# Scores of two heads as float32 products in halves of TensorE's rows, without split keys and queries

## The chip, the cores and the metric

The kernel runs on one core of a Trainium2 chip. A core has TensorE (PE: an array of 128 rows and 128 columns, fed with weights by PEld), VectorE (DVE), ScalarE (ACT), GpSimd (POOL), and DMA queues, which here are all issued by SyncE (SP). The metric is the time on the device in microseconds, and fewer is better. A difference is told in percent of the kernel before.

## The reference

Attention over 2 batches, 8 heads, 576 positions and 64 channels, in which each query keeps only its 32 largest scores, then two feed-forward layers on the 1152 x 512 result, all in float32:

```python
scores = scale * np.matmul(q, k.transpose(0, 1, 3, 2))
kth = np.partition(scores, -top_k, axis=-1)[..., -top_k:-top_k + 1]
scores = np.where(scores >= kth, scores, -1000000000.0)
attn = np.exp(scores - np.max(scores, axis=-1, keepdims=True))
attn = attn / (np.sum(attn, axis=-1, keepdims=True) + 1e-09)
x = np.matmul(attn, v)                 # then (batch x position) x (head x channel)
h = x @ w_in;  x = (h * np.tanh(softplus(h))) @ w_out        # 512 -> 2048 -> 512
h = x @ w2_in; x = (h * sigmoid(h)) @ w2_out                 # 512 -> 2048 -> 512
```

The feed-forward weights come as float64, so they have to be turned into float32 on the chip.

## The kernel before

**Tiles.** The 1152 rows are 9 tiles of 128. Attention goes by tile and by pair of heads, so there are 36 pairs. Tile 4 holds the end of batch 0 and the start of batch 1, so its scores have two parts.

**One pair.** Scores (L391) go to PSUM in four pieces, one for each head and each half of the 576 keys (288 columns), each piece in one of two banks (`ps_att`, `att=2`). ScalarE or VectorE copies a piece into `sc` (L295, L297). VectorE finds the 32 largest of a row by four MAX8 (L407) and three MATCH_REPLACE8 (L410) a head. ScalarE takes the exponential (L423, or L433 and L440 in the last tiles), L427 masks it. TensorE transposes the result (L452, also in `ps_att`), ScalarE copies it to `pt`, and the value products follow (L468 and L471, `ps_misc`): each head writes 64 of the 128 PSUM partitions, that is, it uses 64 columns of the array. L485 turns the reciprocal denominators and L494 multiplies by them into `xt`.

**How scores are made.** A float32 product is two records on TensorE, a product of the shorter type `float32r` one. To keep float32's precision with the shorter type, keys and queries are split in two parts, a rounded one and the remainder. Keys are loaded twice, one copy above the other (`kraw`, both halves of the 128 partitions), copied as `float32r` by ScalarE or VectorE into `kk`, and in the lower 64 partitions the remainder replaces the copy (GpSimd or VectorE, `kraw` minus `kk`). Queries are loaded the same way (`qraw`) and become two tiles in `qs`, rounded and remainder. A product over 128 rows then sums the query part times both key parts, and two products, one for each query part, give one piece of scores:

```python
ops = [(T[K("qs", i)][:, x, h], T["kk", b, p][:, h]) for i, (b, _, _) in enumerate(pp) for x in range(2)]
for i, (l, r) in enumerate(ops):
    nc.tensor.matmul(o, lhsT=l, rhs=r[:, f * SH:(f + 1) * SH], start=(i == 0), stop=(i == len(ops) - 1))
```

In tile 4 each part has its own `qs`, cleared by GpSimd outside its rows (L373), so a piece takes four products. Keys are prepared once for a batch and a pair (8 times), queries 36 times.

**Feed-forward.** Weights arrive as float64 in `wide`, and ScalarE (L519, L531) and GpSimd (L523, L533) make float32 of them in `wraw`. Tiles 0, 1 and 2 go through layer 1 in float32 (`BLOCK1`, mode 'n'), the others in pairs of tiles with split operands (mode 'r'); layer 2 is the same but for tiles 0 and 1 taken together. L735 and L644 are the first products of a layer (`ps_h`), L714 and L821 the second (`ps_y`). Weights are split into `ws` by copy and subtraction (L295, L297, L303, L305).

**The order.** Every step is given to `Plan.add` with the engines that may do it, a cost, and a rank. Ranks come from tables: `TILES` (start and step of a tile's four pairs), `DUE1` and `DUE2` (of the groups of the layers), `OFF` and `FLEX` (offsets for each kind of step and for taking an alternative engine). `Plan.emit` goes through them with its own costs, keeps count of the buffers (`SBUF_BUFS`, `PSUM_BUFS`), and writes each engine's instructions in the order found. On the chip every engine then runs its own list in that order, and waits where what it needs is not there.

## Time and profile before

| | |
|---|---|
| Time, median of 3 runs | 646.25 us (643.49 to 648.09) |
| The profiled execution | 642.01 us, its span 640.2 us |
| TensorE clock granted, mean | 0.989 |
| Busy share: TensorE / its weight loads | 93% / 82% |
| Busy share: VectorE / ScalarE / GpSimd | 82% / 74% / 53% |
| DMA | 178.34 MB, mean 279 GB/s |

The profile shows one execution. "Busy" is the time in which an engine had an instruction running; on TensorE, products are pipelined, so the price of one in a stream is the distance from its start to the next one's, and its own duration is longer. Idle time is given with its releaser: the instruction whose end the waiting one had needed. A float32 product stands as two records (in the order of the program below it is one MATMUL). L numbers are lines of the kernel that ran.

### The profile page before, as it was taken

How to read it: one execution, taken by the hardware profiler on the slowest of the kernel's cores; microseconds unless marked ns; L12 is line 12 of the kernel's file. 1: busy time of each engine (PE TensorE's matmuls, PEld its weight loads, DVE VectorE, ACT ScalarE, POOL GpSimd, SP SyncE). 2: the span in 40 equal slices, each digit the busy share in tenths (PEclk: the TensorE clock that was granted, in tenths of full speed). 3: DMA queues.
4: the chain of work that ended last, by engine and by line, in shares of the span. 5: the costliest groups of instructions: out<-in, count | busy, mean ns of one | idle time of the engine just before them, and what ended most of it. 6: DMA issues, size and time to landing. Idle time of an engine off the chain costs nothing.

```text
span 640.2 us, 13237 instructions
## 1 busy us (share of the span) xinstructions
PE 592.8 (93%) x4616; PEld 527.9 (82%) x4616; DVE 528.0 (82%) x1121; ACT 476.9 (74%) x991; POOL 338.0 (53%) x319
## 2 busy tenths in 40 slices
PE   1587739999999999999999999999999999999997
PEld 1476629999998966788999778999998999989986
DVE  4999999997999999789999989999996244755541
ACT  6899999897699999988997767996895344333321
POOL 6788886671367877877877426448782000000000
PEclk9998988999999999999999999999999999999999
DMA  9978886997798978999799697959669888887661
GB/s 307 298 226 275 278 251 208 341 335 233 237 326 267 309 247 264 302 370 357 266 383 369 219 341 275 317 164 343 223 221 346 329 306 307 284 253 266 238 193 70
DMA packets 85650, 178.34 MB, mean 279 GB/s; under 512 B 8144, under 2 KB 29136, under 8 KB 85584
## 3 DMA queue, kind: packets, MB, share of 16 engines
q1 hardware_dynamic: 85584, 177.50, 81.7%
q8 instruction: 36, 0.59, 0.4%
q14 instruction: 30, 0.25, 0.1%
HBM read 138.94 MB, written 38.54 MB: 277 GB/s over the span
## 4 chain that ended last, share of the span: by engine, by line
PE 73%; ACT 13%; DMA 7%; DVE 4%; POOL 1%; issue 1%; SPq 0%; POOLq 0%; ACTq 0%; DVEq 0%
PE ps_h L644 26%; PE ps_y L714 16%; PE ps_y L821 15%; PE ps_att L391 5%; PE ps_misc L468 5%; ACT ws L519 4%; PE ps_att L452 4%; DMA w2i<-wraw 2%; ACT wraw L531 2%; DVE m L407 2%; DMA wide<-in_w1o_dram 2%; DVE rest L410 2%; DMA qraw<-in_qh_dram 1%; ACT sc L295 1%; ACT pt L295 1%
## 5 line engine op out<-in xcount | busy, mean ns | idle before, releaser
L407 DVE MAX8 m<-rest 128x8 f32<-128x576 f32 x216 | 154.2, 745 | 0.1
L410 DVE MATCH_REPLACE8 rest<-m,rest 128x576 f32<-128x576 f32 x144 | 106.1, 741 | 0.0
L295 ACT CAST ws<-wraw 128x512 fp32r<-128x512 f32 x98 | 60.1, 622 | 55.8 <-PE ps_h L644 25.9
L519 ACT ACTIVATE ws<-wide,zone 128x512 int32<-128x512 int16 x128 | 95.2, 783 | 2.0 <-POOL wraw L533 1.3
L533 POOL TENSOR_TENSOR wraw<-wraw,ws 128x512 int32<-128x512 int32 x64 | 81.6, 1283 | 15.0 <-ACT wraw L531 3.1
L391 PE MATMUL ps_att<-kk,qs 128*128 128x288 f32 x320 | 67.7, 334 | 22.9 <-POOL kk L303 18.5
L523 POOL TENSOR_TENSOR ws<-ws 128x512 int32<-128x512 int32 x64 | 81.8, 1289 | 9.5 <-ACT ws L519 6.3
L303 POOL TENSOR_TENSOR ws<-wraw,ws 128x512 fp32r<-128x512 f32 x52 | 66.6, 1296 | 26.2 <-DVE ws L297 7.4
L391 PEld LDWEIGHTS ps_att<-kk,qs 128*128 128x128 f32 x320 | 49.1, 198 | 32.0 <-POOL kk L303 20.1
L644 PEld LDWEIGHTS ps_h<-y,ws 128*128 128x128 f32 x576 | 72.8, 188 | 3.0 <-issue 0.2
L644 PE MATMUL ps_h<-y,ws 128*128 128x256 f32 x576 | 75.0, 279 | 0.0
L644 PE MATMUL ps_h<-xt,ws 128*128 128x256 f32 x576 | 70.8, 279 | 0.0
L714 PE MATMUL ps_y<-g,ws 128*128 128x256 f32 x540 | 70.1, 280 | 0.0
L644 PEld LDWEIGHTS ps_h<-xt,ws 128*128 128x128 f32 x576 | 68.1, 188 | 0.8 <-issue 0.6
L305 DVE TENSOR_TENSOR ws<-wraw,ws 128x512 fp32r<-128x512 f32 x57 | 41.5, 734 | 30.2 <-ACT ws L295 29.8
L714 PEld LDWEIGHTS ps_y<-g,ws 128*128 128x128 f32 x540 | 65.3, 188 | 0.7 <-issue 0.7
L821 PE MATMUL ps_y<-ws,g 128*128 128x512 f32 x252 | 65.4, 398 | 0.0
L714 PE MATMUL ps_y<-hs,wraw 128*128 128x128 f32 x384 | 51.6, 282 | 7.6 <-ACT bias L419 7.6
L407 DVE MAX8 m<-sc 128x8 f32<-128x576 f32 x72 | 53.0, 746 | 4.2 <-ACT sc L295 4.1
L452 PE MATMUL ps_att<-ident,e 128*128 128x128 f32 x324 | 51.7, 286 | 3.9 <-DVE e L427 2.8
L714 PEld LDWEIGHTS ps_y<-hs,wraw 128*128 128x128 f32 x384 | 48.2, 198 | 8.3 <-POOL wraw L533 7.7
L410 DVE MATCH_REPLACE8 rest<-m,sc 128x576 f32<-128x576 f32 x72 | 53.1, 740 | 0.0
(90 smaller groups left out, 1147.7 us busy)
## 6 DMA issues: line engine op xcount, KB each, us to landing
wraw<-w1i SPq DMA_DIRECT2D x64, 256.0 KB, 4.5
wraw<-w2i SPq DMA_DIRECT2D x64, 256.0 KB, 3.9
ws<-w1o_split SPq DMA_DIRECT2D x30, 512.0 KB, 5.6
ws<-w2o_split SPq DMA_DIRECT2D x28, 512.0 KB, 4.6
wraw<-w1o SPq DMA_DIRECT2D x48, 256.0 KB, 4.9
wide<-in_w1i_dram SPq DMA_DIRECT2D x16, 512.0 KB, 5.6
wide<-in_w1o_dram SPq DMA_DIRECT2D x16, 512.0 KB, 5.0
wide<-in_w2i_dram SPq DMA_DIRECT2D x16, 512.0 KB, 4.8
```

Of the source, the lines that this page charges most:

```text
L295: ways.append(("act", act_us(n, psum), act, lambda: nc.scalar.copy(get_out(), get_in())))
L303: ways.append(("pool", pool_us(n), pool, lambda: nc.gpsimd.tensor_tensor(out=get_out(), in0=get_a(), in1=get_b(), op=op)))
L391: nc.tensor.matmul(o, lhsT=l, rhs=r[:, f * SH:(f + 1) * SH], start=(i == 0), stop=(i == len(ops) - 1))
L407: add([("dve", 0.67, 0, lambda i=i, h=h, src=src: nc.vector.max(out=m8()[:, h, 8 * i:8 * i + 8], in_=src()[:, h]))], reads=srck, writes=[K ...
L410: add([("dve", 0.73, 0, lambda i=i, h=h, src=src: nc.vector.match_replace(out=rest()[:, h], in_to_replace=m8()[:, h, 8 * i:8 * i + 8], in_ ...
L452: nc.tensor.transpose(o[:, i, :], ef[:, (c + i) * P:(c + i + 1) * P], ident)
L519: add([("act", act_us(UNIT) + 0.14, 0, lambda i=i: nc.scalar.activation(pn()[:, i], top(), AF.Relu, scale=ONE16 - 2 * ONE16 * i, bias=zone))],
L523: ways = [("pool", pool_us(UNIT), 0, lambda: nc.gpsimd.tensor_tensor(out=se(), in0=pn()[:, 0], in1=pn()[:, 1], op=ALU.subtract))]
L533: add([("pool", pool_us(UNIT), 0, lambda: nc.gpsimd.tensor_tensor(out=w().bitcast(I32), in0=w().bitcast(I32), in1=se(), op=ALU.add))], rea ...
L644: nc.tensor.matmul(hp[:, c, :], lhsT=l, rhs=rr, start=(i == 0), stop=(i == len(ops) - 1))
L714: nc.tensor.matmul(yp[:, o, :], lhsT=l[:, d * P:(d + 1) * P], rhs=rr[:, c, :], start=(fc == 0 and k == 0 and o == 0), stop=last, skip_grou ...
L821: nc.tensor.matmul(op, lhsT=gg[:, c, i * P:(i + 1) * P], rhs=wt, start=(fc == 0 and k == 0), stop=(fc == NFC - 1 and k == len(ops) - 1))
```

## The change

Keys and queries are no longer split. Queries are loaded once as `q`, 128 partitions: the 64 channels of one head above those of the other. Keys likewise (`kk`, 128 x 576). The tiles `kraw`, `qraw` and `qs` and all steps that filled them are gone: the key and query casts, subtractions, and the clearing for tile 4. The scores of half a row of keys are now one step for both heads: head 0 as a float32 product of the upper 64 rows of the array, head 1 of the lower 64, each into a bank of its own, so one step takes both `ps_att` banks. In tile 4 each part is a product that writes only its own rows of the bank. `sc` has six buffers instead of four, `ws` nine instead of eight. All numbers that set the order are new, and so are the charges of a score step and of a feed-forward product.

```diff
-TILES = [(-38.49, 10.5), (10.1, 9.21), (77.14, -12.91), (164.62, 9.79), (162.43, 9.24), (220.65, 45.49), (300.21,
...
+TILES = [(2.7, 15.05), (53.05, -1.62), (84.54, -8.19), (202.03, -14.5), (188.75, 19.51), (283.83, -8.15), (312.51,
...
-SBUF_BUFS = dict(kraw=1, kk=5, v=5, qraw=2, qs=2, sc=4, rest=1, e=1, pt=2, m8=10, bias=10, den=8, x=3, dt=2, xt=1,
-    wraw=9, ws=8, hs=2, th=1, wide=3, g=3, y=2, o=2)
+SBUF_BUFS = dict(kk=5, v=5, q=3, sc=6, rest=1, e=1, pt=2, m8=10, bias=10, den=8, x=3, dt=2, xt=1, wraw=9, ws=9, hs=2,
+    th=1, wide=3, g=3, y=2, o=2)
...
-            add(copy_ways(S, hi, src, dve="khi", twice=True), reads=[raw + (h,)], writes=[kk + (h, 0)], uses=U,
-                rank=rank - 6, boost="k")
-            add(tt_ways(S, lo, lambda h=h: T[raw][D:, h], lo, ALU.subtract, dve="klo"), reads=[raw + (h,), kk + (h, 0)], writes=[kk + (h, 1)],
-                uses=U, rank=rank - 6, boost="k")
+        for f in ([0], [1]) if b == 0 and p == 0 else ([0, 1],):
+            cs = slice(f[0] * SH, (f[-1] + 1) * SH)
+            add([("sp", 0.06, 0, lambda cs=cs: nc.sync.dma_start(
+                out=get(kk, lambda: sbuf("kk", [P, S]))[:, cs], in_=kh[b, p][:, cs]))],
+                writes=[kk + (i,) for i in f], uses=[(kk, "kk")], rank=rank - 8, boost="kload", load=len(f) * P * SH * 4)
...
-            add(copy_ways(2 * (r1 - r0), hi, raw, dve="qhi", twice=True), reads=[K("qraw")], writes=[q], uses=U,
-                rank=rank - 6, boost="q")
-            add(tt_ways(2 * (r1 - r0), lo, raw, hi, ALU.subtract, dve="qlo"), reads=[K("qraw"), q], writes=[q], uses=U,
-                rank=rank - 6, boost="q")
+        add([("sp", 0.06, 0, lambda: nc.sync.dma_start(out=get(K("q"), lambda: sbuf("q", [P, P])), in_=qh[t, p]))],
+            writes=[K("q")], uses=[(K("q"), "q")], rank=rank - 8, boost="qload", load=P * P * 4)
...
+        for f in range(2):
+            sp = [K("sp", f, h) for h in range(2)]
+
+            def scores(f=f, sp=sp):
+                for b, r0, r1 in pp:
+                    for h in range(2):
+                        rows = slice(h * D, h * D + D)
+                        nc.tensor.matmul(get(sp[h], lambda: psum("att", [P, SH]))[r0:r1], lhsT=T[K("q")][rows, r0:r1],
+                                         rhs=T["kk", b, p][rows, f * SH:(f + 1) * SH], start=True, stop=True, skip_group_check=True)
+            add([("pe", 0.515, 0, scores)], reads=[K("q")] + [("kk", b, p, f) for b, _, _ in pp], writes=sp, rank=rank - 10,
+                boost="sp", uses=[(k, "ps_att") for k in sp] + [(K("q"), "q")] + [(("kk", b, p), "kk") for b, _, _ in pp])
...
-        native, parts = 0.221 * N / P, 0.354 * N / 256
+        native, parts = (0.2225 if N == P else 0.216 * N / P), 0.3475 * N / 256
```

In the changed kernel the lines have moved up: scores stand at L364, transposes at L424, values at L440 and L443, denominators at L457, and the products of the layers at L707 and L616 (`ps_h`), L686 and L793 (`ps_y`).

The first place is the start of TensorE's list, where the first pairs are made. Before, its first rows are:

```order
L391 MATMUL ps_att<-kk,qs 128x288 x16
L452 MATMUL ps_att<-ident,e 128x128 x9
L485 MATMUL ps_att<-ident,x 128x128
L468 MATMUL ps_misc<-pt,v 64x128 x8
L471 MATMUL ps_misc<-pt,v 64x128 x2
L735 MATMUL ps_h<-xt,wraw 128x128 x4
L391 MATMUL ps_att<-kk,qs 128x288 x4
L735 MATMUL ps_h<-xt,wraw 128x128 x4
L391 MATMUL ps_att<-kk,qs 128x288 x4
```

and now:

```order
L364 MATMUL ps_att<-kk,q 128x288 x8
L424 MATMUL ps_att<-ident,e 128x128 x9
L457 MATMUL ps_att<-ident,x 128x128
L440 MATMUL ps_misc<-pt,v 64x128 x8
L443 MATMUL ps_misc<-pt,v 64x128 x2
L364 MATMUL ps_att<-kk,q 128x288 x2
L707 MATMUL ps_h<-xt,wraw 128x128 x8
L364 MATMUL ps_att<-kk,q 128x288 x2
L707 MATMUL ps_y<-xt,wraw 128x128 x8
```

Both begin with the scores of two pairs; a pair was 8 products and is now 4, two for each half row. Later scores come as bursts of two between the first feed-forward products, where four stood together.

The second place is on TensorE too, where the first layer's first products of tile 1 (L644 before, L616 now, `ps_h`) stand with the second ones of tile 0 (L714, now L686) and the scores of a later pair. Before:

```order
L485 MATMUL ps_att<-ident,x 128x128
L714 MATMUL ps_y<-hs,wraw 128x128 x4
L391 MATMUL ps_att<-kk,qs 128x288 x4
L644 MATMUL ps_h<-xt,wraw 128x128 x4
L391 MATMUL ps_att<-kk,qs 128x288 x4
L714 MATMUL ps_y<-hs,wraw 128x128 x4
L644 MATMUL ps_h<-xt,wraw 128x128 x12
L468 MATMUL ps_misc<-pt,v 64x128 x8
L471 MATMUL ps_misc<-pt,v 64x128 x2
```

and now:

```order
L457 MATMUL ps_att<-ident,x 128x128
L686 MATMUL ps_y<-hs,wraw 128x128 x4
L616 MATMUL ps_h<-xt,wraw 128x128 x4
L364 MATMUL ps_att<-kk,q 128x288 x2
L686 MATMUL ps_y<-hs,wraw 128x128 x4
L616 MATMUL ps_h<-xt,wraw 128x128 x4
L364 MATMUL ps_att<-kk,q 128x288 x2
L616 MATMUL ps_h<-xt,wraw 128x128 x4
L686 MATMUL ps_y<-hs,wraw 128x128 x4
```

The scores were two groups of four, each two pieces of a row of one head; now they are two bursts of two, each half a row of both heads, with full-array products ahead of and behind each. The changed list has 188 borders between products of the whole array, of 64 of its columns (values) and of 64 of its rows (scores), where the one before has 72, all at the value products.

## Rows read from the trace of the kernel before

**Rows 1.** The page's part 1: busy us (share of the span) and instructions of each engine.

```profile
PE 592.8 (93%) x4616; PEld 527.9 (82%) x4616; DVE 528.0 (82%) x1121; ACT 476.9 (74%) x991; POOL 338.0 (53%) x319
```

**Rows 2.** Table of stretches: length, then busy (count) by engine, PEclk, DMA share, GB/s.

```profile
8.00:20.00 12.00, 1.81 (x7) 1.14 (x5) 11.30 (x24) 10.28 (x19) 7.68 (x8) 1.00 1.07 375
20.00:95.00 75.00, 52.46 (x372) 42.87 (x372) 73.91 (x164) 73.88 (x157) 63.45 (x57) 0.95 0.85 261
...
104.00:500.00 396.00, 392.58 (x3206) 347.89 (x3204) 366.80 (x800) 335.67 (x727) 253.36 (x236) 1.00 0.85 294
500.00:637.00 137.00, 136.50 (x978) 126.62 (x974) 67.00 (x115) 45.05 (x70) 2.58 (x2) 1.00 0.73 247
```

**Rows 3.** Timeline of TensorE around one value burst: start us, us, instruction, count.

```profile
158.86 1.05 PE L714 MATMUL ps_y<-hs,wraw 128*128 128x128 f32 x8
159.84 1.09 PE L468 MATMUL ps_misc<-pt,v 128*64 128x128 f32 x16
160.77 0.39 PE L471 MATMUL ps_misc<-pt,v 128*64 128x128 f32 x4
161.09 0.80 PE L391 MATMUL ps_att<-kk,qs 128*128 128x288 f32 x4
161.72 0.49 PE L714 MATMUL ps_y<-hs,wraw 128*128 128x128 f32 x3
```

**Rows 4.** Timeline of TensorE, two streams of products from each start to the next.

```profile
164.03 4.63 PE L644 MATMUL ps_h<-xt,wraw 128*128 128x128 f32 x40
168.42 1.30 PE L391 MATMUL ps_att<-kk,qs 128*128 128x288 f32 x8
169.56 1.05 PE L644 MATMUL ps_h<-xt,wraw 128*128 128x128 f32 x8
...
226.75 3.62 PE L644 MATMUL ps_h<-y,wraw 128*128 128x256 f32 x16
230.20 0.97 PE L452 MATMUL ps_att<-ident,e 128*128 128x128 f32 x6
```

**Rows 5.** Groups by line and shape: busy us, mean ns of one | idle us before them.

```profile
L295 ACT COPY sc<-ps_att 128x288 f32<-128x288 f32 x120 | 43.7, 403 | 9.2 <-PE ps_att L391 8.6
...
L303 POOL TENSOR_TENSOR qs<-qraw,qs 128x256 fp32r<-128x256 f32 x32 | 23.4, 733 | 19.9 <-issue 5.6 <-PE ps_y L821 4.8 <-ACT qs L295 4.2
...
L303 POOL TENSOR_TENSOR kk<-kraw,kk 64x576 fp32r<-64x576 f32 x15 | 20.9, 1414 | 5.3 <-DVE e L427 1.5 <-issue 1.2 <-DMA kraw<-in_kh_dram 1.1
...
L295 ACT CAST kk<-kraw 128x576 fp32r<-128x576 f32 x16 | 10.5, 681 | 2.0 <-DMA kraw<-in_kh_dram 1.8
...
L297 DVE COPY sc<-ps_att 128x288 f32<-128x288 f32 x24 | 10.5, 449 | 13.4 <-PE ps_att L391 13.3
...
L373 POOL MEMSET qs<- 128x512 f32 x8 | 4.2, 525 | 21.5 <-PE ps_att L391 21.5
...
L305 DVE TENSOR_TENSOR kk<-kraw,kk 64x576 fp32r<-64x576 f32 x1 | 0.8, 756 | 0.0
```

**Rows 6.** Timeline of the start, all engines, the first pair's way to its first MAX8.

```profile
4.92 1.46 ACT L295 CAST kk<-kraw 128x576 fp32r<-128x576 f32 x2 [1.16 <-DMA kraw<-in_kh_dram]
...
5.73 2.77 POOL L303 TENSOR_TENSOR kk<-kraw,kk 64x576 fp32r<-64x576 f32 x2 [1.07 <-DMA kraw<-in_kh_dram]
...
7.18 1.33 PE L391 MATMUL ps_att<-kk,qs 128*128 128x288 f32 x4 [7.18 <-POOL kk L303]
...
8.06 0.94 DVE L297 COPY sc<-ps_att 128x288 f32<-128x288 f32 x2 [8.06 <-PE ps_att L391]
...
9.04 0.76 DVE L407 MAX8 m<-sc 128x8 f32<-128x576 f32 x1
...
11.20 0.76 DVE L407 MAX8 m<-sc 128x8 f32<-128x576 f32 x1 [0.54 <-ACT sc L295]
```

**Rows 7.** Timeline of TensorE: the eighth pair's denominators, and the last products.

```profile
110.07 0.33 PE L485 MATMUL ps_att<-ident,x 128*128 128x128 f32 x1
...
634.96 1.54 PE L821 MATMUL ps_y<-keep,g 128*128 128x512 f32 x6
```

More of the change, by code (lines that the diff above doesn't have):

```diff
@@ L257 @@
     NPAIR, D = qh.shape[1], qh.shape[2] // 2
-    S = kh.shape[4]
+    S = kh.shape[3]
     NFC = w1i.shape[0]
@@ L323, in load_kv @@
         kk, vv = ("kk", b, p), ("v", b, p)
-        raw = ("kraw", b, p)
-        first = b == 0 and p == 0
-        for h in ([0], [1]) if first else ([0, 1],):
-            hs = slice(h[0], h[-1] + 1)
-            add([("sp", 0.06, 0, lambda hs=hs: nc.sync.dma_start(
-                out=get(raw, lambda: sbuf("kraw", [P, 2, S]))[:, hs], in_=kh[b, p][:, hs]))],
-                writes=[raw + (i,) for i in h], uses=[(raw, "kraw")], rank=rank - 8, boost="kload", load=len(h) * P * S * 4)
-        for h in range(2):
-            hi = lambda h=h: get(kk, lambda: sbuf("kk", [P, 2, S], F32R))[:, h]
-            lo = lambda h=h: T[kk][D:, h]
-            src = lambda h=h: T[raw][:, h]
-            U = [(raw, "kraw"), (kk, "kk")]
-            add(copy_ways(S, hi, src, dve="khi", twice=True), reads=[raw + (h,)], writes=[kk + (h, 0)], uses=U,
-                rank=rank - 6, boost="k")
-            add(tt_ways(S, lo, lambda h=h: T[raw][D:, h], lo, ALU.subtract, dve="klo"), reads=[raw + (h,), kk + (h, 0)], writes=[kk + (h, 1)],
-                uses=U, rank=rank - 6, boost="k")
+        for f in ([0], [1]) if b == 0 and p == 0 else ([0, 1],):
[3 more added lines that the diff above has]
+                writes=[kk + (i,) for i in f], uses=[(kk, "kk")], rank=rank - 8, boost="kload", load=len(f) * P * SH * 4)
         add([("sp", 0.06, 0, lambda: nc.sync.dma_start(out=get(vv, lambda: sbuf("v", [P, NB + 1, D])), in_=va[b, p]))],
@@ L365, in attention @@
         K = lambda name, *rest: (name,) + key + rest
-        add([("sp", 0.06, 0, lambda: nc.sync.dma_start(out=get(K("qraw"), lambda: sbuf("qraw", [P, 2, P])), in_=qh[t, p]))],
-            writes=[K("qraw")], uses=[(K("qraw"), "qraw")], rank=rank - 8, boost="qload", load=P * P * 8)
-        for i, (b, r0, r1) in enumerate(pp):
-            q = K("qs", i)
-            mk = lambda x=slice(0, 2), q=q: get(q, lambda: sbuf("qs", [P, 2, 2, P], F32R))[:, x]
-            if len(pp) > 1:
-                add([("pool", 0.5, 0, lambda mk=mk: nc.gpsimd.memset(mk().bitcast(F32), 0.0))], writes=[q], uses=[(q, "qs")],
-                    rank=rank - 6)
-            raw = lambda r0=r0, r1=r1: T[K("qraw")][:, :, r0:r1]
-            hi, lo = (lambda x=x, mk=mk, r0=r0, r1=r1: mk(x)[:, :, r0:r1] for x in range(2))
-            U = [(q, "qs"), (K("qraw"), "qraw")]
-            add(copy_ways(2 * (r1 - r0), hi, raw, dve="qhi", twice=True), reads=[K("qraw")], writes=[q], uses=U,
-                rank=rank - 6, boost="q")
-            add(tt_ways(2 * (r1 - r0), lo, raw, hi, ALU.subtract, dve="qlo"), reads=[K("qraw"), q], writes=[q], uses=U,
-                rank=rank - 6, boost="q")
@@ L382, in attention @@
-        sc = lambda: get(K("sc"), lambda: sbuf("sc", [P, 2, S]))
-        for h in range(2):
-            for f in range(2):
-                sp = K("sp", h, f)
-                def scores(h=h, f=f, sp=sp):
-                    o = get(sp, lambda: psum("att", [P, SH]))
-                    ops = [(T[K("qs", i)][:, x, h], T["kk", b, p][:, h]) for i, (b, _, _) in enumerate(pp) for x in range(2)]
-                    for i, (l, r) in enumerate(ops):
-                        nc.tensor.matmul(o, lhsT=l, rhs=r[:, f * SH:(f + 1) * SH],
-                                         start=(i == 0), stop=(i == len(ops) - 1))
-                add([("pe", 0.276 * len(pp), 0, scores)],
-                    reads=[K("qs", i) for i in range(len(pp))] + [("kk", b, p, h, x) for b, _, _ in pp for x in range(2)],
-                    writes=[sp], rank=rank - 10, boost="sp",
-                    uses=[(sp, "ps_att")] + [(K("qs", i), "qs") for i in range(len(pp))] + [(("kk", b, p), "kk") for b, _, _ in pp])
-                add(copy_ways(SH, lambda h=h, f=f: sc()[:, h, f * SH:(f + 1) * SH], lambda sp=sp: T[sp], dve="sc", psum=True),
-                    reads=[sp], writes=[K("sc", h, f)], uses=[(sp, "ps_att"), (K("sc"), "sc")], rank=rank - 10, boost="sc")
```

37 lines of the change are left out of this document (18 added, 19 removed).

## The prediction, made before the changed kernel ran

> **What bounds the kernel now.** I read the page's engine totals first, then a table of stretches, then single stretches of TensorE's timeline. The totals [rows 1] show TensorE busy for 93% of a span of 640.2 us and VectorE for 82%, with ScalarE and GpSimd behind. One total says nothing of where the limit lies, so the table of stretches comes next [rows 2]: from 8 to 20 us TensorE works 1.81 of 12 us and from 20 to 95 us 52.46 of 75, while VectorE works 11.30 and 73.91. So up to about 95 us VectorE's top-32 search sets the pace and TensorE waits for its results. From 104 to 500 us TensorE is busy 392.58 of 396 us, from 500 to 637 us 136.50 of 137: it is the limit for the other five sixths, and VectorE there has room (366.80 of 396, then 67.00 of 137). A busy TensorE is not one at its peak, so I check the rate: 40 float32 records of 128 columns stand from 164.03 to 168.42 us, 110 ns each [rows 4], which is their streaming price. What TensorE has to stream, plus what it loses between streams, is the time from about 100 us on.
>
> The border between the two regimes is taken at the eighth pair (tile 1, last pair of heads), whose denominators TensorE turns at 110.07 us; the last products stand at 634.96 us [rows 7]. After that border TensorE has about 525 us of nearly gapless work. The change therefore counts in two sums: how much earlier VectorE brings the eighth pair, and how much more or less TensorE has to do after it.
>
> **Part 1: the start.** Today keys arrive at about 4.92 us, are copied by ScalarE (0.68 us) and reduced by GpSimd (1.41 us a half), the first scores start at 7.18 us, the first MAX8 at 9.04 and the second head's at 11.20 after 0.54 us of idle VectorE [rows 6]. The change takes copy and subtraction away; if the keys land as today (one more query load stands ahead of them, but each load is half as large), scores start 2.26 us earlier. Behind that the chain gets a little longer: each half row now fills both score banks at once, so the second half waits until both copies are out. With today's 0.88 us from the first score to its copy, and 0.45 us a copy [rows 5, 6], I get 4.92 + 0.88 + 0.45 + 0.88 + 0.45 = 7.58 us for the first MAX8, 1.5 us earlier than 9.04. Both heads are then ready together, which saves the 0.54 us. Up to the eighth pair VectorE also loses three copies of scores (5 before, 2 now, and both of these precede the first MAX8; before, 2 of 5 did) and the one key subtraction it did: 3 x 0.449 + 0.756 = 2.1 us [rows 5]. Of its 1.09 us idle between 20 and 95 us I count half. Sum: 1.5 + 0.5 + 2.1 + 0.5 = **4.6 us earlier**. Bounds: 2.1 (only VectorE's own work shrinks) and 6 (keys land sooner and all idle goes).
>
> ScalarE and GpSimd lose all key and query parts: 10.5 us and 20.9 us for keys, 23.4 us for most of the queries on GpSimd, 4.2 us of clearing [rows 5]. I cost this at nothing in the first 100 us, because VectorE is full there and is what is waited for. It is not nothing for conversions: the weights' conversion gets done sooner, which fills idle TensorE time that is idle either way.
>
> **Part 2: the price of a score burst on TensorE.** After the border the old kernel has 240 score products of 288 columns, one record each. Eight in a row stand from 168.42 to 169.56 us [rows 4]; the first one behind a float32 stream takes some 0.08 us more, which that stream gives back at its end, so one costs (1.14 - 0.08) / 8 = 0.1325, say 0.134 us with the change of stream: 240 x 0.134 = 32.2 us. A float32 product is two records of two passes: 110 ns for 128 columns, and 16 records of 256 columns from 226.75 to 230.20 us give 216 ns [rows 4], so 0.84 ns a column and 242 ns for 288. No row shows a product in 64 rows of the array. The nearest ones are the value products, which use 64 columns of the array: 16 records from 159.84 to 160.77 us, 58 ns each against 110 ns in the full array [rows 3]. Two of them run side by side. I take that for halves by rows too: a burst (two heads, half a row of keys) costs 2 x 0.242 = 0.484 us. After the border there are 44 such bursts, and 8 of four products in the tile that holds the end of one batch and the start of the other; I count those two at a time, 0.968 us. 44 x 0.484 + 8 x 0.968 = 29.0 us: **3.2 us less**. If all four of the mixed tile run at once it is 7.1 less; if nothing runs side by side it is 44 x 0.968 + 8 x 1.936 = 58.1, 25.9 us more.
>
> **Part 3: what each change of form costs.** This is the term that the diff hides. In the timeline around one value burst [rows 3] eight full-array records of 110 ns start at 158.86 and should be through at 159.74; the burst starts at 159.84. Its last four records start at 160.77 and at 54.5 ns each are through at 160.99; the next full-array product starts at 161.09. Each border costs about 0.10 us (I use 0.095) in which TensorE streams nothing, though it counts as busy. Besides, the first weights behind a border are not loaded ahead: 16 records take 0.93 instead of 0.87 us, and the four score products behind the burst take 0.63 instead of 0.53. A whole excursion costs about 0.10 + 0.05 + 0.10 + 0.10 = 0.35 us.
>
> The page "TensorEngine Tiling (Array Packing)" of the Trainium skill, section "Key Properties", says that a change of tiling mode drains TensorE; the trace agrees for halves by columns, at these 0.10 us, and by that rule the new score bursts drain too.
>
> The old kernel has 56 such borders after the eighth pair (28 value bursts); in the new one, going down TensorE's rows and counting values, scores and the rest as three forms, there are 152, since nearly every score burst stands alone between full-array work. That is 96 more, or 48 excursions. Bounds: 0 if a half by rows needs no drain, 48 x 0.35 = 16.8 us if it pays all that a value burst pays. I take the two drains and not the loads: the drain appears at the value burst whatever stands around it, the uncovered load differs with the instruction that comes next. 96 x 0.095 = **9.1 us more**. In the start, before the border, TensorE has the time and this costs nothing.
>
> **Part 4: waits.** From 104 to 500 us TensorE idles 3.4 us [rows 2]. ScalarE, GpSimd and VectorE all get lighter (VectorE copies 16 half rows of scores instead of 24), so I let it go: -3.4. Against it, scores now claim both banks: eight bursts after the border stand only four float32 products (8 x 0.110 = 0.88 us) behind the burst before them, and two copies of 0.40 us on ScalarE with their signals take about 1.1, so 8 x 0.2 = +1.6. Net **1.8 less**; bounds 3.4 less and 1.6 more. In the other bursts over 1.1 us of other products covers the copies; without that cover each would wait about a microsecond. DMA loses 2.3 MB of queries and 2.4 MB of keys of 178 and was not waited for here.
>
> **Sum.** -4.6 - 3.2 + 9.1 - 1.8 = -0.5 us: 640.2 becomes 639.7. The profiled execution took 642.0 us, its span 640.2, and the median of the runs shown is 646.25, which is 0.9% above the span; scaled alike, 639.7 gives 645.7 us. So I forecast **no change**: the work removed was mostly on engines that TensorE doesn't wait for, and TensorE pays for narrower products with drains about what the start gains.
>
> **Rivals.**
> *No drain for halves by rows.* Then part 3 is zero: -4.6 - 3.2 - 1.8 = -9.6, span 630.6, 636.6 us on the median's scale. For it: both heads keep all 128 columns and only the rows are split, and no row shows such a product. Against it: all borders around value bursts that I looked at pay.
> *The whole excursion is paid.* Slower. Place: TensorE at each lone score burst after the border. Price 0.35 us x 48 = 16.8, and the waits of part 4 stay as they are: -4.6 - 3.2 + 16.8 = +9.0, span 649.2, 655.3 us. It decides above 0.16 us an excursion, where the gains of parts 1 and 2 are used up. For it: the weights of a 64-row product have 128 columns, and the load seen uncovered in front of 128 columns is the larger one (0.10 against 0.05).
> A rule of the skill speaks for it: the page "TensorE: Matmul & The Clock Gate", section "The mechanism" of Part 3, says that a weight load overlaps running products only where the row group differs, and a full-array product uses all of them.
> *The two heads don't run side by side.* Part 2 becomes +25.9: -4.6 + 25.9 + 9.1 - 1.8 = +28.6, span 668.8, 675 us. Against it: the value products do overlap, and the two heads write different banks.
> *VectorE stays the limit longer* or the conversions become it: only if the start gains nothing, which is inside the bounds of part 1.
>
> **Chances.** Forecast 0.38, no drain 0.33, whole excursion 0.20, one after the other 0.07, anything else 0.02. About 1%, 6.5 us, is what a measurement can tell from no change here. Below 639.8 us lie the no-drain case nearly whole and the lower edge of the forecast: faster 0.36. Above 652.7 lie most of the whole excursion and all of the serial case: slower 0.27. The rest, 0.37, is the same. The range leaves out the serial case and the tails of two others: 632 (no drain, with some 4 us from the mixed tile) to 657 (whole excursion with a weaker start). The forecast alone, with part 1 and 4 at their bounds, is 642 to 652.
>
> **What would show it.** Right: the first MAX8 near 7.6 us; the eighth pair's denominators turned near 105 us; score records of about 242 ns in pairs a few ns apart; about 0.10 us lost at each border of a score burst; TensorE still busy over 98% from 104 us on; about 136 us of TensorE work behind the last value burst, as in today's last stretch. Wrong: score records that start 240 ns apart without partners (serial), a score burst whose next product follows with no loss (no drain), TensorE idle of several us after 110 us with copies of scores as releaser, or an eighth pair that is not earlier.

## The result, and the profile after

The changed kernel takes 650.69 us (median of 10 runs, 648.64 to 652.31), the one before 645.65 us beside it (10 runs, 643.49 to 650.44). The ratio is 1.0071, with a 95% interval of 1.0044 to 1.0097: slower by 0.7%, about 5 us. I had forecast 645.7 us, no change. The time lies inside the range given (632 to 657), but it is not the result that was forecast, and the sum behind the forecast lacks a term, as the experiments show.

The profiled execution took 649.6 us, its span 647.8 us against 640.2. The page's totals of the changed kernel (columns as in [rows 1]):

```profile
PE 613.7 (95%) x4616; PEld 514.1 (79%) x4616; DVE 497.7 (77%) x1063; ACT 462.6 (71%) x944; POOL 337.2 (52%) x304
```

The work went where the diff says: against [rows 1] VectorE lost 30 us of busy time, ScalarE 14, and TensorE, the engine that sets the time, gained 21. Its table of stretches (columns as in [rows 2]):

```profile
8.00:20.00 12.00, 3.84 (x12) 2.22 (x13) 12.00 (x26) 8.94 (x18) 1.32 (x2) 1.00 0.96 331
20.00:95.00 75.00, 60.55 (x402) 45.63 (x401) 73.69 (x165) 73.80 (x152) 59.27 (x52) 0.89 0.83 259
...
104.00:500.00 396.00, 395.22 (x3107) 325.92 (x3108) 342.70 (x749) 322.29 (x682) 245.66 (x219) 1.00 0.82 276
500.00:637.00 137.00, 137.00 (x993) 128.42 (x992) 59.63 (x100) 45.91 (x76) 24.60 (x19) 1.00 0.78 269
```

TensorE now idles 0.8 us between 104 and 500 us, where [rows 2] had 3.4: the waits went. The time is lost while TensorE is "busy". The eighth pair's denominators (L457) and the last products, as in [rows 7], with the products around the first:

```profile
104.78 0.33 PE L457 MATMUL ps_att<-ident,x 128*128 128x128 f32 x1
...
642.54 1.52 PE L793 MATMUL ps_y<-keep,g 128*128 128x512 f32 x6
```

That pair is 5.3 us earlier than the 110.07 of before, and TensorE's last record starts at 643.7 (it is the last of the six), where the one before had its at 636.1: behind the border TensorE needs 538.9 instead of 526.0 us, **12.9 us more**. The prediction's sum for this part was +4.1.

Two views show where these 12.9 us may come from. First a lone score burst, TensorE's timeline of the changed kernel (L364 scores, L616 and L686 feed-forward), and one of the mixed tile:

```profile
159.80 0.39 PE L616 MATMUL ps_h<-xt,wraw 128*128 128x128 f32 x2
160.12 0.76 PE L364 MATMUL ps_att<-kk,q 64*128 64x288 f32 x4
160.80 8.30 PE L616 MATMUL ps_h<-xt,wraw 128*128 128x128 f32 x72
168.94 0.82 PE L424 MATMUL ps_att<-ident,e 128*128 128x128 f32 x6
...
208.09 1.06 PE L686 MATMUL ps_y<-hs,wraw 128*128 128x128 f32 x8
209.08 0.72 PE L364 MATMUL ps_att<-kk,q 64*64 64x288 f32 x8
209.73 1.16 PE L686 MATMUL ps_y<-hs,wraw 128*128 128x128 f32 x8
```

The two records at 159.80 should be through at 160.02, and the burst starts at 160.12: 0.10 us to drain. Its four records run in twos, one head beside the other (their starts are 7 ns apart), and should stream for 0.484 us, but the next product starts 0.68 us later: the second pair starts 0.35 us behind the first instead of 0.24, which I put down to its weights, and 0.10 is the drain at the end. And the 72 records behind it take 8.14 us, 0.11 more than their 111.5 ns each. A lone burst costs 0.885 us, 0.40 more than its stream. This one is typical: in all 44 bursts of four records behind the border the next product starts 0.69 us after the burst's first, and the median price with what is lost on either side is 0.88 us. In the mixed tile (eight records, L364 with 64 columns) all four products run at once: 0.65 us to the next start, 0.85 with both borders. The second view is a stretch that the change does not touch at all, 144 split products of the first layer near the end, in the kernel before and then in the changed one, each with the row behind it:

```profile
504.55 16.48 PE L644 MATMUL ps_h<-xt,ws 128*128 128x256 f32 x144
520.87 1.52 PE L714 MATMUL ps_y<-g,ws 128*128 128x256 f32 x12
```

```profile
509.20 17.44 PE L616 MATMUL ps_h<-xt,ws 128*128 128x256 f32 x144
526.48 1.60 PE L686 MATMUL ps_y<-g,ws 128*128 128x256 f32 x12
```

The same 144 records take 16.32 us before and 17.28 after: 113.3 and 120.0 ns each, at a granted clock of 1.00 in both. There are 1692 records of this kind (`float32r`, 256 columns, weights from `ws`) behind the border. The first nine experiments weigh the bursts and the order, the last seven this second view.

### The profile page after: what moved, and what is told of

Same layout as the page of the kernel before. It is cut to its first block, busy times and chain, and to the rows that moved or that the text cites. A ratio compares the mean times of both kernels' runs of the same rounds, so it can differ in the third digit from the quotient of the medians.

```text
span 647.8 us, 13074 instructions
## 1 busy us (share of the span) xinstructions
PE 613.7 (95%) x4616; PEld 514.1 (79%) x4616; DVE 497.7 (77%) x1063; ACT 462.6 (71%) x944; POOL 337.2 (52%) x304
## 4 chain that ended last, share of the span: by engine, by line
PE 86%; ACT 8%; DVE 2%; DMA 2%; issue 1%; SPq 0%; ACTq 0%
PE ps_h L616 33%; PE ps_y L686 17%; PE ps_y L793 17%; PE ps_att L364 7%; PE ps_misc L440 5%; PE ps_att L424 5%; ACT ws L491 3%; DMA wide<-in_w1i_dram 1%; PE ps_misc L443 1%; ACT wraw L503 1%; ACT sc L293 1%; DVE m L379 1%; ACT pt L293 1%; ACT e L395 1%; DVE rest L382 1%
## 5 line engine op out<-in xcount | busy, mean ns | idle before, releaser
L293 ACT CAST ws<-wraw 128x512 fp32r<-128x512 f32 x103 | 62.5, 623 | 65.6 <-PE ps_h L616 37.7
L382 DVE MATCH_REPLACE8 rest<-m,rest 128x576 f32<-128x576 f32 x144 | 106.2, 742 | 0.0
L301 POOL TENSOR_TENSOR ws<-wraw,ws 128x512 fp32r<-128x512 f32 x58 | 73.9, 1291 | 19.4 <-ACT ws L293 10.5
L616 PE MATMUL ps_h<-xt,ws 128*128 128x256 f32 x576 | 76.8, 289 | 0.0
L616 PE MATMUL ps_h<-y,ws 128*128 128x256 f32 x576 | 76.5, 283 | 0.0
L616 PEld LDWEIGHTS ps_h<-y,ws 128*128 128x128 f32 x576 | 73.9, 191 | 2.3
L616 PEld LDWEIGHTS ps_h<-xt,ws 128*128 128x128 f32 x576 | 71.1, 191 | 5.2 <-issue 4.3
L686 PE MATMUL ps_y<-g,ws 128*128 128x256 f32 x540 | 73.8, 287 | 0.0
L364 PE MATMUL ps_att<-kk,q 64*128 64x288 f32 (+1 forms) x320 | 61.5, 475 | 10.7 <-ACT sc L293 5.5
L686 PEld LDWEIGHTS ps_y<-g,ws 128*128 128x128 f32 x540 | 67.2, 191 | 4.9 <-issue 4.4
L301 POOL TENSOR_TENSOR g<-th,g 128x512 fp32r<-128x512 f32 x23 | 29.8, 1295 | 77.1 <-DVE g L295 76.3
L793 PE MATMUL ps_y<-ws,g 128*128 128x512 f32 x252 | 64.7, 396 | 0.0
L424 PE MATMUL ps_att<-ident,e 128*128 128x128 f32 x324 | 51.7, 285 | 13.7 <-DVE e L399 9.7
L293 ACT COPY sc<-ps_att 128x288 f32<-128x288 f32 x128 | 46.1, 407 | 19.4 <-PE ps_att L364 18.0
L424 PEld LDWEIGHTS ps_att<-ident,e 128*128 128x128 f32 x324 | 38.4, 145 | 25.8 <-POOL ws L495 8.4
L293 ACT COPY pt<-ps_att 128x384 f32<-128x384 f32 x108 | 48.6, 484 | 11.7 <-PE ps_att L424 8.9
L686 PE MATMUL ps_y<-hs,wraw 128*128 128x128 f32 x384 | 52.7, 288 | 4.3 <-ACT hs L655 4.3
```

Source lines behind the costliest of these rows:

```text
L293: ways.append(("act", act_us(n, psum), act, lambda: nc.scalar.copy(get_out(), get_in())))
L301: ways.append(("pool", pool_us(n), pool, lambda: nc.gpsimd.tensor_tensor(out=get_out(), in0=get_a(), in1=get_b(), op=op)))
L364: nc.tensor.matmul(get(sp[h], lambda: psum("att", [P, SH]))[r0:r1], lhsT=T[K("q")][rows, r0:r1], rhs=T["kk", b, p][rows, f * SH:(f + 1) * ...
L382: add([("dve", 0.73, 0, lambda i=i, h=h, src=src: nc.vector.match_replace(out=rest()[:, h], in_to_replace=m8()[:, h, 8 * i:8 * i + 8], in_ ...
L424: nc.tensor.transpose(o[:, i, :], ef[:, (c + i) * P:(c + i + 1) * P], ident)
L616: nc.tensor.matmul(hp[:, c, :], lhsT=l, rhs=rr, start=(i == 0), stop=(i == len(ops) - 1))
```

## Experiments

Three theories are named in the expectations. **D**: the borders around score bursts cost the 12.9 us. **O**: the new order does. **A**, from e10 on: the place of `ws` in memory does, in part. In batches, the kernel before ran on the same chip beside them (646.2, 647.2, 647.3, 646.5 and 645.9 us).

**Taking the borders away.** In the changed kernel, all 128 rows for the 32 pairs outside the mixed tile:

```diff
-                        rows = slice(h * D, h * D + D)
+                        rows = slice(h * D, h * D + D) if len(pp) > 1 else slice(0, P)
```

> The changed kernel, with each score product of the 32 unmixed pairs taken over all 128 rows of the array in float32 (so each piece holds the sum of both heads' scores, and the output is not the reference's); order, buffers and all else as in the changed kernel. Theory D (drains: a lone burst in halves of rows costs 0.885 us, of which 0.40 are two drains and two weight loads that are not hidden): a burst without change of form takes 4 x 0.242 = 0.968 us, 44 bursts after the eighth pair x 0.083 = +3.7 us on the changed kernel's span of 647.8: 651 to 653. Theory O (a burst costs its stream of 0.484 us, the loss comes from the new order and from both score banks being taken at once): 44 x 0.484 = +21 us, about 669.

Measured: 657.84 us, ratio to before 1.0189 (1.0154 to 1.0224). TensorE's timeline:

```profile
159.82 0.65 PE L364 MATMUL ps_att<-kk,q 128*128 128x288 f32 x2
160.31 1.05 PE L686 MATMUL ps_y<-hs,wraw 128*128 128x128 f32 x8
161.20 1.14 PE L364 MATMUL ps_att<-kk,q 128*128 128x288 f32 x4
162.17 1.05 PE L686 MATMUL ps_y<-hs,wraw 128*128 128x128 f32 x8
```

Four records in 0.97 us and eight in 0.89: no border is left, and the burst is 0.085 us dearer than the half-row one with its borders. 44 of them make 3.7 us; behind the border the kernel needs 543.6 us, 4.7 more than the changed one. So a half-row burst keeps little of the gain of running two heads at once: 0.97 without halves, 0.885 with them, 0.484 if borders were free. The remaining 2.9 us lie in the start (denominators at 107.7), which I had costed at nothing; with them the span is 655.4 us, above the 651 to 653 of theory D and far below the 669 of theory O.

The same with one pass, on the upper 16 bits of keys and queries (less exact), short diff:

```diff
+                as_ = ... x.bitcast(mybir.dt.bfloat16).rearrange("p (n t) -> p n t", t=2)[:, :, 1]
-                ... lhsT=T[K("q")][rows, r0:r1], rhs=T["kk", b, p][rows, ...]
+                ... lhsT=as_(T[K("q")])[rows, r0:r1], rhs=as_(T["kk", b, p])[rows, ...]
```

> As the run over the full array, but with the upper halves of the float32 words of queries and keys as bfloat16, one pass a product (output not the reference's): same order, same claims of both banks, no change of form for the 32 unmixed pairs. A burst should take about 2 x 0.125 = 0.25 us. Theory D: 44 x (0.885 - 0.25) = -28 us on 647.8, about 620 where TensorE stays the limit, up to 628 if VectorE becomes it. Theory O: 44 x (0.484 - 0.25) = -10 us, about 638, with the waits of the new order still there.

Measured: 630.71 us, ratio 0.976 (0.9734 to 0.9787); 519.1 us behind the border, 19.8 less than the changed kernel, where 44 bursts of 0.26 us instead of 0.885 would give 27.5; TensorE has new waits there, 2.6 us of them for ScalarE's copies of scores, which is not all of the difference. The time lies between what the two theories expected, nearer to D's. TensorE's time is what counts, and the start (105.0) does not suffer here.

**Adding borders to the kernel before.** A product of two columns over 64 rows ahead of the first head's scores of each half row, 70 in all and 52 behind the border:

```diff
+                    if h == 0:
+                        nc.tensor.matmul(o[:, :2], lhsT=ident[:D], rhs=ident[:D, :2], start=True, stop=True, ...)
```

> The kernel before, with one tiny float32 product of 64 rows and two columns put ahead of the first head's scores of each half row (the scores overwrite it): 70 excursions into halves of rows with nothing in them, 52 of them after the eighth pair, order unchanged. Theory D: 52 x (0.40 + about 0.05 for the product itself) = +23 us on 640.2, about 663 (ratio 1.035). Theory O: only the products themselves, 52 x 0.05 = +3 us, about 643.

And its control, the same with `lhsT=ident, rhs=ident[:, :2]`, over all rows:

> The kernel before, with the same extra product of two columns ahead of the first head's scores of each half row as in e3_empty_excursions, but over all 128 rows of the array: no change of form, everything else the same; its result is overwritten by the scores that follow. Theory D (the drains and the uncovered weight loads at a change of form are what costs): only the product itself and its weight load are paid, some 0.06 to 0.12 us each for the 52 after the border, 3 to 6 us, and a few in the start; the last TensorE product comes 526 + 3 to 6 us after the eighth pair's denominators, the time is 647 to 656 us. Rival (any extra product at these 70 places costs as much, by its order and its wait for the bank): as e3_empty_excursions, 670 to 680 us.

Measured: 675.42 us, ratio 1.0452 (1.0406 to 1.0499), and 656.0 us, ratio 1.0118 (1.0076 to 1.016). Behind the border 549.6 and 536.4 us, 23.6 and 10.4 more than the 526.0. The timelines of TensorE, of the half-row one and then of the control:

```profile
134.33 1.06 PE L716 MATMUL ps_y<-hs,wraw 128*128 128x128 f32 x8
135.31 0.38 PE L391 MATMUL ps_att<-ident 64*128 64x2 f32 x2
135.62 0.53 PE L393 MATMUL ps_att<-kk,qs 128*128 128x288 f32 x2
```

```profile
129.47 1.06 PE L716 MATMUL ps_y<-hs,wraw 128*128 128x128 f32 x8
130.37 0.28 PE L391 MATMUL ps_att<-ident 128*128 128x2 f32 x2
130.51 0.51 PE L393 MATMUL ps_att<-kk,qs 128*128 128x288 f32 x2
130.86 0.28 PE L391 MATMUL ps_att<-ident 128*128 128x2 f32 x2
```

In halves the tiny product comes 0.09 us after the stream ahead of it is through and holds the array for 0.31 us; over all rows it comes at once and holds it for 0.14. My expectation of 3 to 6 us for the control was too low: weight loads start 0.11 us apart there, two columns hide none, and such a product costs 0.2 us. So theory D's forecast for the half-row run (23 us, measured 23.6) was met partly by luck: it had put 0.05 us of each on the product itself. The 13.2 us between the two are what 102 changes of form cost (158 behind the border instead of 56), 0.13 us each with the loads that they uncover. That a change of form costs is shown; it does not show that it is all of the 12.9 us.

**The order.** The changed kernel with the tables of before, and with the charges of a score step and a value step at the measured prices (0.885; 1.44 and 1.80):

```diff
-TILES = [(2.7, 15.05), (53.05, -1.62), (84.54, -8.19), ...
+TILES = [(-38.49, 10.5), (10.1, 9.21), (77.14, -12.91), ...
```

> The changed kernel with the order tables of the kernel before (TILES, DUE1, DUE2, FLEX, FLEX1, EARLY, OFF); the form of the scores, six sc buffers, nine ws buffers and the charges stay as changed. It also has 152 borders between forms after the eighth pair, and the same 52 score bursts. Theory D (the form of the scores costs the 13 us after the border): last TensorE product 537 to 545 us after the eighth pair's denominators, as the 538.9 of the changed kernel and not the 526.0 of the one before; the time is 646 to 656 us, with the start's gain depending on the order. Theory O (the new order costs it): after the border 526 us or a little less, the time 632 to 640 us.

```diff
-            add([("pe", 0.515, 0, scores)], ...
+            add([("pe", 0.885, 0, scores)], ...
```

> The changed kernel with the planner's charges for a score step and a value step set to what the trace of the changed kernel shows (0.885 us instead of 0.515; 1.44 and 1.80 instead of 1.25 and 1.32), so that only the order is made otherwise. Theory D: there are again 152 borders after the eighth pair, so TensorE's work after it stays at 537 to 541 us; the time is within 5 us of the changed kernel's 650.7. Theory O (the order went wrong because the planner thought the bursts cheaper than they are): some 8 to 13 us come back, 638 to 643 us.

Measured: 682.13 us (ratio 1.0535, 1.0481 to 1.0588) and 661.44 us (1.0221, 1.0164 to 1.0278), both outside what either theory expected. With the old tables TensorE needs 566.6 us behind the border and waits there (7.7 us for an exponential on ScalarE alone); with the new charges the eighth pair comes at 113.7 us instead of 104.8, and TensorE then needs 541.6 us, although `ws` happens to lie where its products are fast (see below). Neither order gives back anything, and the changed kernel waits less than the one before (TensorE idle 0.8 us against 3.4 from 104 to 500 us), so nothing is left for theory O as a loss by waiting. That another order, with fewer borders, could do better is not tested. These runs don't weigh D: any edit to costs or ranks moves many steps, and tables fitted to other numbers fit it badly.

**Taking the start's gain alone.** In the kernel before, the new form of scores for tiles 0 and 1, for tile 0, and for the first pair only (its scores straight from `kraw` and `qraw`):

```diff
+        whole = t < WHOLE
-            load_kv(b, p, rank)
+            (load_whole if whole else load_kv)(b, p, rank)
```

> The kernel before with its own order tables, in which only tiles 0 and 1 (eight pairs, ahead of the point where TensorE becomes the limit) make their scores in the new way, without split; tiles 2 to 8 as before. Theory D: the start gains what the changed kernel gained there (eighth pair's denominators 5.3 us earlier) and no score burst pays drains after it: 640.2 - 5 = 635 (ratio 0.990 to 0.995), faster than both. Theory O (the start gain belongs to the new order): 640, ratio 1.00.

> The kernel before with tile 0 alone in the new form (its four pairs; whole keys and queries), split keys and queries from tile 1 on, the tables of before. If four pairs of split keys can be made beside tile 1's search without holding VectorE up, the eighth pair comes at 106 to 109 us, the 526 us behind it stay, and the time is 638 to 644 us. If the keys' preparation holds tile 1 up, as it held up tile 2 in e4_early_tiles_only, the eighth pair comes at 112 us or later and the time is 648 us or more.

> The kernel before with one thing of the change: the first pair's scores (tile 0, heads 0 and 1) are float32 products of 64 rows straight from the loaded keys and queries, each piece of a head a product of its own; the pair's queries are not split; everything else, split keys too, is as before. Part 1 of the prediction alone: the first scores start near 4.6 us instead of 7.18, the first MAX8 near 7 instead of 9.04, and the second head's search waits for nothing; with VectorE full up to 95 us the eighth pair's denominators come 2 us earlier (108 instead of 110), TensorE's 526 us behind them stay, and the time is 2 us less (ratio 0.997). If the start's gain comes only from VectorE's own work getting less (fewer copies and subtractions), the eighth pair stays at 110 us and the time is the same.

Measured: 664.35 us (1.0287, 1.0244 to 1.033), 670.55 us (1.0372, 1.033 to 1.0413) and 658.16 us (1.0189, 1.0146 to 1.0232): all three missed. The first pair's search does start earlier in the last one (7.61 instead of 9.04 us), but the eighth pair comes at 113.7, 111.6 and 113.6 us and more time is lost behind it (548.4, 552.3 and 536.5 us), as with the other edits to the plan; in the first two `ws` had also moved to its slow place. The hoped-for mixture of both kernels was not found.

**The place of the split weights.** The plan's first use of a buffer decides where it lies. Before, `ws` begins 32 bytes past a multiple of 128 in a partition; in the changed kernel it comes behind `bias`, and begins 96 past one. The operands that run against it (`xt`, `y`, `g`) lie at 96 in both. No trace shows addresses: these are worked out from the sizes of the buffers, taken in the order of their first use. In the first nine experiments the rate went with it: 120 ns where `ws` was at 96 (e1, e2, e4, e6, e9), 113 to 118 where it was at 32 (e3, e5, e7, e8). Unused bytes move `ws` alone, with order and work untouched:

```diff
+        if first:
+            sb.tile([P, 16], F32, name="ahead", bufs=1)
         t = sb.tile(shape, dtype, tag=tag, ...)
+        if first:
+            sb.tile([P, 16], F32, name="behind", bufs=1)
```

> The changed kernel with 64 unused bytes a partition ahead of the buffers of `ws` and 64 behind them, so that only the split weights lie elsewhere: at 32 bytes past a multiple of 128, as in the kernel before, instead of at 96. Order, work and everything else are the same. Theory A (the place of the weights sets the rate of the split products: in the traces so far the median distance of the 256-column records from `ws` is 113 to 118 ns in the five kernels with `ws` at 32, and 120 ns in the six with it at 96): these records come at 113 to 118 ns again; 1640 of them after the border, 4 ns each, give back 6.6 us: time 644 us, ratio to the changed kernel 0.990. Theory D alone (the whole 13 us are score bursts and their borders): 120 ns stay, 650 us.

> The kernel before with `ws` moved from 32 to 96 bytes past a multiple of 128, by unused bytes as in e10_ws_moved, and nothing else. Theory A: its 256-column records from `ws` come at 120 ns, the time rises by 6 to 7 us to 652 (ratio 1.010). Theory D alone: no change, 646.

> The changed kernel with `ws` at a multiple of 128 bytes, by 32 unused bytes ahead and 96 behind, nothing else moved. No run so far has it there. If the rate goes by how many pieces of memory a row of weights touches, it is at least as fast as at 32: records at 113 ns or less throughout and 640 to 644 us; if 32 is special, 120 ns and 650 us.

> The kernel before with `ws` at a multiple of 128 bytes, nothing else moved. If a multiple of 128 is as good as 32: 646 us, the same. If it is better (113 ns for all 256-column records instead of 113 to 118, about 2.5 ns on 1640): 642 us, and this is the better kernel of the two. If the place doesn't matter: 646 us.

> The changed kernel with 64 unused bytes ahead of the buffers of `e`, so that all that lie behind them (`wraw`, `ws`, `pt`, `xt`, `hs`, `y`, `g`, `keep`) move from 96 to 32 bytes past a multiple of 128; order and work are the same. If the place of the loaded weights alone counts (`ws`, as in e10_ws_moved): 113 to 118 ns for the records from `ws` and 646 us; where other weights or the moving operands count too, less, 640 to 644. If weights and moving operands must lie differently (in e10_ws_moved 32 against 96): 120 ns and 651 us.

> The kernel before with 64 unused bytes ahead of the buffers of `e`: `pt`, `xt`, `hs`, `y`, `g` and `keep` move from 96 to 32, while `ws` and `wraw` are at 32 already and stay. If only the place of `ws` counts: 646 us, the same. If moving operands count as weights do: 640 to 643 us, better than both. If weights and moving operands must lie differently: 652 us.

> The changed kernel with `ws` alone at 64 bytes past a multiple of 128. Of the other places 32 was fast (646.3 us), 0 and 96 slow (651.4, 650.7). If 32 alone is good: 650 to 652 us. If the distance from the moving operands (which lie at 96) counts, as in 64 for `ws` at 32: 32 away, as 0 is, and slow too.

| run | kernel | `ws` at | moving operands at | us of the 144 records | ns each | time, us | ratio to before |
|---|---|---|---|---|---|---|---|
| (before) | before | 32 | 96 | 16.32 | 113.3 | 645.65 | 1 |
| e11 | before | 96 | 96 | 17.28 | 120.0 | 651.21 | 1.0074 (1.0041 to 1.0107) |
| e13 | before | 0 | 96 | 17.28 | 120.0 | 651.64 | 1.0078 (1.004 to 1.0116) |
| e15 | before | 32 | 32 | 17.28 | 120.0 | 650.66 | 1.0054 (1.0027 to 1.0081) |
| (changed) | changed | 96 | 96 | 17.28 | 120.0 | 650.69 | 1.0071 (1.0044 to 1.0097) |
| e10 | changed | 32 | 96 | 16.32 | 113.3 | 646.28 | 1.0007 (0.9979 to 1.0034) |
| e12 | changed | 0 | 96 | 17.28 | 120.0 | 651.35 | 1.0075 (1.0049 to 1.01) |
| e14 | changed | 32 | 32 | 17.27 | 119.9 | 650.08 | 1.006 (1.0038 to 1.0082) |
| e16 | changed | 64 | 96 | 16.81 | 116.7 | 646.78 | 1.0003 (0.9979 to 1.0028) |

The same stretch in e10, then in e11 and in e14 (timelines of TensorE, each with the next row):

```profile
507.30 16.48 PE L625 MATMUL ps_h<-xt,ws 128*128 128x256 f32 x144
523.62 1.52 PE L695 MATMUL ps_y<-g,ws 128*128 128x256 f32 x12
```

```profile
510.65 17.44 PE L653 MATMUL ps_h<-xt,ws 128*128 128x256 f32 x144
527.93 1.60 PE L723 MATMUL ps_y<-g,ws 128*128 128x256 f32 x12
```

```profile
509.08 17.44 PE L621 MATMUL ps_h<-xt,ws 128*128 128x256 f32 x144
526.35 1.60 PE L691 MATMUL ps_y<-g,ws 128*128 128x256 f32 x12
```

With 64 bytes of nothing ahead of `ws` the changed kernel is as fast as the one before; the same bytes make the kernel before as slow as the changed one. It is not the place of `ws` alone: at 32 it is fast against operands at 96 (e10) and slow against operands at 32 (e14, e15). Of the four distances tried, modulo 128, operands that lie 32 or 64 past the weights are fast, 0 or 96 slow; only the distance 0 was tried with two pairs of places, so that it is the distance that counts is the simplest reading and not shown. The float32 products from `wraw` are no part of it: `wraw` lies at 32 before and at 96 in the changed kernel and in e10, and their median distance is 112 ns for 128 columns in all three. Theory A holds for 5 us of the 12.9 (5.2 by e10; the way back, e11, has 6.5). Why the place counts is not shown. The loads' own rows give little of it, a mean of 191 ns in the changed kernel and 188 in e10 (weight loads by line: busy us, mean ns, idle before):

```profile
L616 PEld LDWEIGHTS ps_h<-xt,ws 128*128 128x128 f32 x576 | 71.1, 191 | 5.2 <-issue 4.3 <-POOL xt L301 0.5 <-ACT sc L293 0.2
```

```profile
L625 PEld LDWEIGHTS ps_h<-xt,ws 128*128 128x128 f32 x576 | 69.1, 188 | 5.0 <-issue 4.6 <-ACT sc L302 0.2
```

The eighth pair's denominators and the last products of e10:

```profile
106.16 0.33 PE L466 MATMUL ps_att<-ident,x 128*128 128x128 f32 x1
...
638.73 1.54 PE L802 MATMUL ps_y<-keep,g 128*128 128x512 f32 x6
```

Its last record starts at 639.9 us, 533.7 behind the first row, where the changed kernel has 538.9. None of the versions beats both kernels: e10, e16 and the kernel before are level.

## Why the prediction was wrong

Put together from spans: 640.2 - 5.3 (start) + 12.3 (score bursts) + 5.2 (place of `ws`: 538.9 behind the border in the changed kernel, 533.7 in e10) - 4.6 (what remains, 2.6 of it idle time) = 647.8 us. The prediction had -4.6, +5.9, nothing and -1.8.

**What failed: the sum had no term for products that the change leaves alone.** I priced feed-forward as unchanged, by its rate of before, and all rivals too moved only work that the diff names. The change of order and of buffers moved `ws` by 64 bytes modulo 128, and 1692 products came out slower. That is 5.2 us of the 8.1 by which the span, 647.8, missed the 639.7 of the sum. With `ws` put back (e10) the ratio is 1.0007, and the forecast was 0.999, but that this agrees is luck: the bursts came out 6.4 us dearer than forecast, and a start that by medians gains some 3 us more than forecast (below), with a rest that gains 2.8 us more, nearly made up for it.

**Part 3 was mis-sized, too.** It took two drains (0.19 us an excursion) and left out the uncovered loads. Measured is 0.40 for a lone burst and 0.36 in the mixed tile: both drains, 0.10 inside the burst ahead of the second pair (0.05 in the mixed tile, whose weights have 64 columns instead of 128), 0.10 ahead of the second product behind it. That these are weight loads is read from these distances. 44 x 0.885 + 8 x 0.845 = 45.7 us against 32.2 before, less some 1.2 for ten bursts that stand straight beside value bursts (one border instead of two), is +12.3; I had -3.2 + 9.1 = +5.9. The price that I gave the rival of the whole excursion, 0.35, was nearly right, and its time (649.2 of span) is close to the 647.8, but for the wrong sum: it kept the waits and knew nothing of `ws`. My reason against the loads ("differs with the instruction that comes next") was wrong: the 0.10 us inside the burst are lost in each of the 44, whatever stands around it.

The rule of the Trainium skill that spoke for it (page "TensorE: Matmul & The Clock Gate", section "The mechanism" of Part 3: a load overlaps running products only where the row group differs) agrees with the burst, whose second pair uses the row groups of the first and starts 0.35 us behind it instead of 0.24. The full-array streams use all row groups too and lose nothing between records (110 ns each in [rows 4]); the same section of the Trainium skill names a second case in which a load goes ahead, into the background weight buffer, and which case holds where no run here shows. So the rule gives the sign, and the price is the trace's.

**Part 2** was right for the 44 bursts: pairs 7 ns apart, no serial heads, and 242 ns a record (as e1 shows over the whole array; inside a burst it is 0.35 us with the loss in front of the second pair). For the mixed tile the other bound held, four at once (by its own terms 7.0 us less, not 7.1).

**Part 4** was right in direction and too small: idle of TensorE from 104 to 500 us fell from 3.4 to 0.8 us, and the waits for both banks that I had priced at +1.6 do not appear. Behind the border 4.6 us less remain after the bursts and `ws`; 2.6 are this idle, the rest is spread over transposes and values and not settled.

**Part 1** was right in size against the profiled execution: the eighth pair at 104.8 where I had said near 105. The way there was not quite: the first scores start at 4.48 us, not 4.92, but the first copy comes 1.34 us behind them, not 0.88 (two float32 records of each head come first), so the first MAX8 starts at 8.16, not 7.58; both heads' searches then follow without a gap, as expected. The start rows of the changed kernel, as in [rows 6]:

```profile
4.48 1.33 PE L364 MATMUL ps_att<-kk,q 64*128 64x288 f32 x4 [4.48 <-DMA kk<-in_kh_dram]
...
5.82 0.40 ACT L293 COPY sc<-ps_att 128x288 f32<-128x288 f32 x1 [3.82 <-PE ps_att L364]
...
8.16 1.42 DVE L379 MAX8 m<-sc 128x8 f32<-128x576 f32 x2
```

The execution of before that I read was an early one (642.01 us, where the median beside the changed kernel is 645.65). In e11, e13 and e15, which keep its order, the eighth pair comes at 113.0, 115.0 and 115.0 us, while the changed form has it between 104.6 and 106.2 us in all five traces (the changed kernel, e10, e12, e14, e16). (Products from `ws` begin at about 280 us; the conversions write to it earlier, but in e15 it has not moved.) So I estimate the start's gain at about 8 us by medians rather than 5, which would be why the medians differ by 5 and the spans by 7.6. Rows of e13, from 20 to 104 us (columns as in [rows 2]):

```profile
20.00:60.00 40.00, 29.45 (x211) 23.89 (x212) 38.62 (x85) 37.44 (x81) 32.06 (x28) 1.00 0.80 250
60.00:80.00 20.00, 16.29 (x99) 13.18 (x99) 17.58 (x41) 17.81 (x40) 15.17 (x15) 0.68 0.77 241
80.00:95.00 15.00, 11.97 (x65) 8.96 (x63) 12.14 (x28) 13.11 (x31) 10.49 (x11) 0.73 0.68 222
95.00:104.00 9.00, 3.18 (x15) 3.21 (x16) 9.00 (x23) 8.85 (x15) 7.47 (x8) 0.50 0.59 204
```

TensorE works 29.45 of 40 us up to 60 us at 1.00; then the granted clock is 0.68, a mixture of the two levels, and from 95 to 104 us, where it works 3.18 us, it is 0.50, the lower one (1.2 GHz); VectorE, which I had taken to be full there, works 17.58 of 20 and 12.14 of 15 us and waits: from 20 us to the eighth pair its multiplication into `xt` waits 5.3 us for TensorE's products, where in the kernel before it waited 0.6. So what I called free for TensorE in the start is not; its products can be late, and the search behind them too. In e1 (+2.9 us in the start) this wait is 1.3 us and in e3 (+10.3 us) 6.9. That it is the lower clock that makes them late is not shown: in the changed kernel the granted clock is 0.74 from 40 to 60 us, and VectorE works 19.84 of the 20.

## What to carry to other kernels

Price a product in part of the array with its borders: two drains and every weight load that has nothing to hide behind, here 0.40 us of loss for 0.48 us of work, and gather such products before making more of them. Where a kernel is bound by weight-loading products, compare the rate of streams that the edit does not touch, record for record, before explaining the difference by the edit; a changed order or buffer list also moves every buffer behind it. A kernel whose order comes from fitted tables is hard to mend by a local edit: the five edits of the plan tried here (e4, e6 to e9) came out 11 to 31 us slower than the kernels that they edit.

## What was not expected of the hardware

The rate of full-array `float32r` products whose weights are loaded anew for 256 columns depends on where the weights and the moving operands lie: in a steady stream 113.3 ns with the operands 64 bytes past the weights modulo 128, 116.7 with 32, 120.0 with 0 and with 96, about 5 us of 646; 64, 0 and 96 were seen in both kernels. Four products of 64 rows and 64 columns run at once in quarters of the array (eight float32 records of 288 columns in 0.65 us with the drain behind them). And a product of two columns over the whole array costs 0.2 us (10.4 us for 52), about the time of its two weight loads, which start 0.11 us apart.
